# All four batches' projections by Strassen's product, one batch behind the attention; the cluster mask of the first six pairs as a one-hot product on TensorE

## The chip, the cores and the metric

The kernel runs on one core of a Trainium2 chip, in one launch. The metric is the device time of an execution in microseconds (us), lower is better. TensorE, VectorE, ScalarE, GpSimd and SyncE appear in the profile as PE (its weight loads as PEld), DVE, ACT, POOL and SP; a q behind a name (SPq, POOLq) is the engine's DMA queue.

## The reference, cut to what matters

```python
# q, k, v: (4, 8, 768, 64) float32; centroids: (8, 16, 64) float32
q_n = q / (norm(q) + 1e-6); k_n = ...; c_n = ...          # unit vectors
q_assign = argmax(einsum('bhsd,hcd->bhsc', q_n, c_n)); k_assign = ...
mask   = q_assign[:, :, :, None] == k_assign[:, :, None, :]
scores = where(mask, (q @ k.T) / sqrt(64), -1e9)
attn   = softmax(scores)                                   # row by row
x = (attn @ v), heads side by side                         # (3072, 512)
h = x @ w_in                                               # w_in  (512, 2048) float64
g = h - tanh(h)
out = g @ w_out                                            # w_out (2048, 512) float64
```

A query attends only to the keys of its own cluster. The weights arrive as 64-bit floats, two 32-bit words each, and the kernel makes float32 of them itself.

## The kernel before, in words

**Attention.** Two heads make a pair, one on partitions 0 to 63 and one on 64 to 127; four batches of four pairs make 16 pairs. Of a pair, the 768 queries are taken in two halves of 384, and the 768 keys in six blocks of 128. Two key blocks are one *step*, so there are 3 steps in a half, 6 in a pair, 24 in a batch and 96 in all. A step's work: eight score matmuls (`score`, L327; a float32 matmul has two records in the trace), an exponential of both blocks on ACT in place in PSUM (L332), the cluster mask on DVE (`select`, L341: exponential times "query's code equals key's code", from PSUM into the SBUF tile `e`), sums of `e` over the keys on Pool (L350 for the first two blocks, L354 twice in each later step), and the product with the values on PE (`value`, L363). There are two PSUM buffers for scores and two for `e`.

**Ends of a half.** `take` copies the result from PSUM (L386), `total` multiplies Pool's sums by ones on PE (L396), ACT adds an epsilon (L400), Pool adds to a check tile (L401, `wholes`), `divide` takes the reciprocal in three parts on DVE (L407), multiplies (L410), and Pool adds to another check tile (L411, `inverses`). In the first half of batch 0 (`early`) Pool sums nothing: PE multiplies `e` by ones in every step (L372).

**Stages of the next pair.** q and k are loaded, transposed on PE (L248) and copied on ACT (L255); similarities to the centroids (L267, L272), transposes (L280), four DVE operations that give each row a cluster code (L286 to L293), a transpose and a cast of the queries' codes (L302, L306), a DMA that writes them to DRAM (L308), and one for each half that spreads them over all partitions (L315, tile `row`).

**Projections.** One batch's attention runs while the projections of the batch before run between its instructions. For batch 0 they are plain products: `plain_items(0)` and `plain_items(1)` for the two halves of the queries, up (L424), tanh (L429), difference (L431), down (L439). To begin early, batch 0 takes all first halves (steps 0 to 11) and then all second halves (12 to 23); half 0 is projected in steps 12 to 23 and half 1 in steps 24 to 47. Batches 1 to 3 use Strassen's product with seven multiplications for eight: `up_pair` (L599, then DVE additions L585, tanh L589, Pool L590, L623, L624) and `down_product` (L641, DVE L652, Pool L648, L661). Batch 1 is projected in steps 48 to 71, batch 2 in 72 to 95, and batch 3 after the last step (the tail).

**Weights.** `weights_on` turns 32 pieces of 512 KB into float32 during the first 24 steps: a DMA on Pool's queue (L164), ACT (L120), and three DVE operations (`assemble`: L121, L125, L128). They stay in SBUF until batch 0 is projected. From step 24 on, `up_maker` and `down_maker` form the sums of Strassen's factors on DVE (L516) and write all factors to DRAM; they are streamed back for each batch (L538). From step 48 on, the weights are read again for a range check (L732, L742).

The order is written out by hand: `steps` lists the steps, `fills` which projection runs beside them, `ready` the stages of later pairs, `makers` the factor work, and `todo` holds a step's small work, dealt out between the items of the projection by `between`. In one turn of the loop PE gets the next step's scores first, then this step's values:

```python
            if following:
                begin(following)
            value(n, half, s)
```

Of the kernel before, what the change touches and what calls it, by code (L numbers as in the profile page):

```python
# [30 lines left out]
F32 = mybir.dt.float32  # L31
# [20 lines left out]

@with_exitstack
def kernel(
# [42 lines left out]
    smallest = const.tile([P, 2 * len_pieces], F32, name="smallest")  # L97
    flag = const.tile([1, 1], I32, name="flag")
# [13 lines left out]

    def assemble(dst, raw, rest):
# [5 lines left out]
        lo, hi = pair[:, :, 0], pair[:, :, 1]  # L119
        nc.scalar.activation(out=rest, in_=lo, func=ACT.Copy, scale=2.0**-29)  # L120
# [9 lines left out]
    def fast():  # L130
# [4 lines left out]
        codep = cx.enter_context(tc.tile_pool(name="codep", bufs=6))  # L135
        qbp = cx.enter_context(tc.tile_pool(name="qbp", bufs=3))
# [8 lines left out]
        first = ExitStack()  # L145
        vp0 = first.enter_context(tc.tile_pool(name="vp0", bufs=2))
        turnp0 = first.enter_context(tc.tile_pool(name="turnp0", bufs=2))
        wp = first.enter_context(tc.tile_pool(name="wp", bufs=1))
        gp = first.enter_context(tc.tile_pool(name="gp", bufs=CF // 2))
        thp = first.enter_context(tc.tile_pool(name="thp", bufs=2))  # L150
        outp = first.enter_context(tc.tile_pool(name="outp", bufs=2))
        rawp = first.enter_context(tc.tile_pool(name="rawp", bufs=3))
        w_in = [wp.tile([P, CD, FQ * P], F32, name=f"w_in{i}") for i in range(NQ4)]
        w_out = [wp.tile([P, FQ, DM], F32, name=f"w_out{i}") for i in range(NQ4)]
        PIECES = pieces(w_in, w_out)
        raws = {}

        def fetch_weights(n: int):
            dst, src = PIECES[n]
            if words == 1:  # L160
                nc.gpsimd.dma_start(dst, src)
                return
            raws[n] = rawp.tile([P, 2 * FQ * P], U32, name="raw")
            nc.gpsimd.dma_start(raws[n], src)  # L164

        def round_weights(n: int):
            if words == 1:
                return
            rest = outp.tile([P, FQ * P], U32, name="rest", tag="osb")
            assemble(PIECES[n][0], raws.pop(n), rest)  # L170

        def constants():
            make_identity(nc, ident)
            nc.vector.memset(ones, 1.0)
            nc.vector.memset(inverses, 0.0)
            nc.vector.memset(wholes, 0.0)
            for c in range(C):
                nc.vector.memset(down[:, c : c + 1], float(C - c))

        cen = const.tile([P, D], F32, name="cen")  # L180
# [4 lines left out]
        def centroid_norms():  # L185
# [7 lines left out]
            nc.scalar.sqrt(nrm, ss)  # L193

# [25 lines left out]


# [3 lines left out]
        def load(n: int, what=(0, 1)):  # L225
# [3 lines left out]
            for i in what:  # L229
                if i < 2 and b == 0:  # L230
                    t = raw_qk[n, i] = gp.tile([P, NCH, 2, D], F32, name=f"x{i}", tag="g")
                elif i < 2:
                    t = raw_qk[n, i] = loads.tile([P, NCH, 2, D], F32, name=f"x{i}")
                else:
                    pool = vp0 if n in (2, 3) else vp
                    t = vals[n] = pool.tile([P, 2, NCH, D], F32, name="vals")
# [6 lines left out]
        def turn(n: int, i: int, engine):  # L243
# [8 lines left out]
            pool = turnp0 if n in (2, 3) else turnp  # L252
            t = turned[n, i] = pool.tile([P, 2, TB], F32, name=f"t{i}")
# [43 lines left out]

        def publish(n: int):

            G = HCH * 4  # L300
            ps = ps_f.tile([G, P], F32, name="pq", tag="f")
            nc.tensor.transpose(  # L302
                out=ps, in_=codes[n][:, 0].rearrange("p a h j -> p (a h j)"), identity=ident
# [75 lines left out]
        def early(n: int, half: int):  # L379

            return n < HP and half == 0
# [684 lines left out]
```

## Time and profile before

| what | value |
|---|---|
| median of 3 runs (lowest, highest) | 1077.87 us (1077.58, 1079.89) |
| the profiled execution, its own time | 1080.79 us |
| its span in the profile, instructions | 1078.9 us, 11996 |
| PE, DVE, ACT, POOL busy | 1007.2, 622.4, 300.7, 551.6 us |
| granted TensorE clock, mean | 0.982 |
| moved by DMA | 124.68 MB |

The profile shows one execution. Busy times are unions of an engine's instructions; the idle time of an engine that doesn't set the pace costs nothing. Matmuls overlap each other, so the mean duration of one is longer than the time that it adds.

### The profile page before, as it was taken

Reading aid. Unit: us, or ns where it says so; the run is one execution under the profiler, and the core shown is the slowest. Engines: PE = TensorE matmul, PEld = TensorE weight load, DVE = VectorE, ACT = ScalarE, POOL = GpSimd, SP = SyncE. Lnnn points to the kernel's source line nnn. Section 1 sums busy time; section 2 is a strip of 40 time slices with the busy share of each in tenths; the row PEclk is TensorE's granted clock in tenths of the full one; section 3 lists DMA queues with packets and bytes.
Section 4 is the critical chain, followed back from the end, with each engine's and each line's share of the span. In section 5 each row is a group of like instructions: output and inputs, shape, how many; then the busy total and the mean of one; then the engine's idle time right before and its main releaser. Section 6 shows DMA issues by size and latency. Waiting matters only on the chain.

```text
span 1078.9 us, 11996 instructions
## 1 busy us (share of the span) xinstructions
PE 1007.2 (93%) x4258; PEld 557.9 (52%) x4258; DVE 622.4 (58%) x1100; ACT 300.7 (28%) x458; POOL 551.6 (51%) x398
## 2 busy tenths in 40 slices
PE   4787998999999999999999999999999999799996
PEld 2332444444444444444456666544456666456885
DVE  5688999335776757656655546655754435544011
ACT  3443433223343323333232221333242211122000
POOL 1012454344655555576678435576778535446701
PEclk9899999999999999999999999999999999899999
DMA  9342343104253352543453454534221222223320
GB/s 261 106 115 84 115 139 93 47 18 124 81 162 108 117 178 89 185 136 112 135 170 131 146 164 141 164 115 144 101 101 49 98 88 74 92 74 112 127 93 32
DMA packets 101603, 124.68 MB, mean 116 GB/s; under 512 B 55328, under 2 KB 80928, under 8 KB 98848
## 3 DMA queue, kind: packets, MB, share of 16 engines
q1 hardware_dynamic: 94576, 100.73, 30.3%
q0 software_dynamic: 6816, 23.07, 6.5%
q8 instruction: 36, 0.59, 0.2%
q14 instruction: 31, 0.25, 0.1%
q10 hardware_dynamic: 144, 0.03, 0.0%
HBM read 102.79 MB, written 21.02 MB: 115 GB/s over the span
## 4 chain that ended last, share of the span: by engine, by line
PE 75%; DVE 10%; issue 7%; POOL 3%; SPq 2%; ACT 2%; DMA 1%; POOLq 0%; DVEq 0%; ACTq 0%
PE pu L599 19%; PE pd L641 14%; PE sc L327 12%; PE av L363 11%; PE o L439 8%; PE h L424 6%; DVE e L341 3%; SPq L238 2%; PE den L396 2%; PE pt L248 2%; PE sim L267 1%; DVE den L407 1%; DVE w_out L125 1%; PE den L372 1%; POOL G L661 1%
## 5 line engine op out<-in xcount | busy, mean ns | idle before, releaser
L341 DVE SCALAR_TENSOR_TENSOR e<-row,code,sc 128x384 f32<-128x384 bf16 x384 | 211.6, 608 | 124.4 <-ACT sc L332 105.2
L354 POOL TENSOR_TENSOR sum<-sum,e 128x768 f32<-128x768 f32 x112 | 207.9, 1856 | 94.4 <-DVE e L341 90.1
L332 ACT ACTIVATE sc<-sc 128x768 f32<-128x768 f32 x192 | 145.1, 790 | 202.1 <-PE sc L327 201.2
L641 PE MATMUL pd<-stream,G 128*128 128x256 f32 x864 | 193.9, 382 | 1.4 <-POOL G L590 1.4
L641 PEld LDWEIGHTS pd<-stream,G 128*128 128x128 f32 x864 | 162.0, 190 | 36.1 <-issue 12.0
L327 PE MATMUL sc<-t,t 64*128 64x384 f32 x768 | 156.6, 519 | 25.1 <-DVE e L341 22.7
L363 PE MATMUL av<-e,vals 128*64 128x384 f32 x768 | 149.5, 512 | 0.0
L599 PE MATMUL pu<-xT,stream 128*128 128x384 f32 x384 | 138.9, 498 | 0.0
L590 POOL TENSOR_TENSOR G<-G,th 128x768 f32<-128x768 f32 x48 | 86.5, 1822 | 89.5 <-ACT th L589 85.1
L327 PEld LDWEIGHTS sc<-t,t 64*128 64x128 f32 x768 | 66.4, 187 | 100.2 <-issue 63.9
L599 PEld LDWEIGHTS pu<-xT,stream 128*128 128x128 f32 x384 | 71.7, 192 | 59.3 <-issue 11.2
L599 PE MATMUL pu<-diff,stream 128*128 128x384 f32 x288 | 101.0, 486 | 0.3 <-DVE diff L565 0.3
L350 POOL TENSOR_TENSOR sum<-e 128x768 f32<-128x768 f32 x28 | 53.6, 1916 | 80.1 <-DVE e L341 80.1
L363 PEld LDWEIGHTS av<-e,vals 128*64 128x64 f32 x768 | 47.7, 139 | 90.0 <-issue 88.2
L424 PE MATMUL h<-xT,w_in 128*128 128x384 f32 x256 | 89.8, 502 | 3.2 <-DVE g L431 3.2
L407 DVE RECIPROCAL den<-den 128x128 f32<-128x128 f32 x96 | 83.1, 915 | 8.2 <-POOL wholes L401 8.2
L439 PE MATMUL o<-w_out,g 128*128 128x512 f32 x192 | 87.6, 602 | 0.0
L589 ACT ACTIVATE th<-G 128x768 f32<-128x768 f32 x48 | 39.8, 843 | 149.2 <-DVE G L585 140.6
L599 PEld LDWEIGHTS pu<-diff,stream 128*128 128x128 f32 x288 | 54.2, 190 | 38.2 <-DVE diff L565 1.0
L424 PEld LDWEIGHTS h<-xT,w_in 128*128 128x128 f32 x256 | 47.6, 192 | 45.1 <-issue 8.7
L657 POOL DMA_DIRECT2D out_dram<-c x36 | 19.9, 554 | 83.9 <-DVE c L652 83.6
L411 POOL TENSOR_TENSOR inverses<-inverses,den 128x384 f32<-128x384 f32 x32 | 41.5, 1297 | 37.6 <-DVE den L407 36.7
(100 smaller groups left out, 867.0 us busy)
## 6 DMA issues: line engine op xcount, KB each, us to landing
stream<-up_factors SPq DMA_DIRECT2D x24, 896.0 KB
stream<-down_factors SPq DMA_DIRECT2D x21, 1024.0 KB
raw<-in_moe_w_in_dram POOLq DMA_DIRECT2D x16, 512.0 KB, 4.5
raw<-in_moe_w_out_dram POOLq DMA_DIRECT2D x16, 512.0 KB, 4.3
again<-in_moe_w_in_dram SPq DMA_DIRECT2D x32, 256.0 KB
again<-in_moe_w_out_dram SPq DMA_DIRECT2D x32, 256.0 KB
x<-in_q_dram SPq DMA_DIRECT2D x32, 192.0 KB
x<-in_k_dram SPq DMA_DIRECT2D x32, 192.0 KB
```

The source lines that it names most:

```text
L327: nc.tensor.matmul(sc[:, h, 0:TB], lhsT=turned[n, 1][r].rearrange("p a n -> p (a n)")[:, j * P : (j + 1) * P], rhs=turned[n, 0][r, half], ...
L332: nc.scalar.activation(out=sc[:, :, 0:TB], in_=sc[:, :, 0:TB], func=ACT.Exp, scale=SCALE)
L341: nc.vector.scalar_tensor_tensor(out=e[:, h], in0=rows[n, half][:, h], scalar=codes[n][:, 1, j // HCH, h, j % HCH : j % HCH + 1], in1=sc[: ...
L350: nc.gpsimd.tensor_tensor(out=s, in0=pair[:, 0], in1=pair[:, 1], op=ALU.add)
L354: nc.gpsimd.tensor_tensor(out=s, in0=s, in1=pair[:, i], op=ALU.add)
L363: nc.tensor.matmul(avs[n, half][h * D : h * D + D], lhsT=vals[n][:, h, j], rhs=e[:, i, h], start=(j == 0), stop=(j == NCH - 1),)
L407: nc.vector.reciprocal(out=t[:, c], in_=t[:, c])
L424: nc.tensor.matmul(h, lhsT=w_in[i][:, c, o * P : (o + 1) * P], rhs=xT[c][:, half], start=(c == 0), stop=(c == CD - 1),)
L439: nc.tensor.matmul(acc[sub], lhsT=gs[f % HF][:, f // HF, sub * P : (sub + 1) * P], rhs=w_out[f // FQ][:, f % FQ], start=(f == sequence[0]) ...
L590: nc.gpsimd.tensor_tensor(out=g[:, f].rearrange("p a n -> p (a n)"), in0=g[:, f].rearrange("p a n -> p (a n)"), in1=th.rearrange("p a n -> ...
L599: nc.tensor.matmul(ps, lhsT=streams[base + i][:, k_, c], rhs=right[which][c], start=(c == 0), stop=(c == CH - 1),)
L641: nc.tensor.matmul(ps, lhsT=left[:, i], rhs=t[:, i], start=(i == 0), stop=(i == HF - 1))
```

## The change

- Batch 0 also goes through Strassen's product. `plain_items`, `early` and the half-by-half order of batch 0 go. Batch b is projected in the 24 steps of batch b + 1 for b = 0, 1, 2, batch 3 in the tail. Steps 0 to 23 have no projection beside them. `fetch_factors` streams factors for all four batches.
- The 32 pieces are rounded and summed as eight units, during the two calls before the loop and steps 0 to 26 (`MADE`): `round_piece` (two raw buffers in place of three), `sum_of`, and one `keep` for each unit, which stores seven factors in one DMA in a new layout.
- For the first six pairs (`masked`) the select on DVE goes. The codes of queries and keys are both spread over the partitions; `one_hot` makes 1 where a query's code is the partition's, and -2^100 where a key's code is not; a bf16 product of the two is added to the scores in PSUM, and the exponential writes straight to `e`.
- Pool sums `e` in all halves, batch 0's first ones too. The rows of a pair are spread once, not once for each half.
- G, the left factors and the late pools are split in two halves that are opened at different times; two Pool subtractions in the down products become two each.
- At the start `keep_warm` runs matmuls of zeros, and the weights' first DMAs wait (`gate`) for pair 0's k. In the tail two more up products come before the transpose of the check's result. The check also reads q and k of the first six pairs again (`largest`).

The diff, cut to its core:

```diff
+MASKED = 6
+FAR = 2.0**100
...
+        def keep_warm(times: int):
+            ps = ps_f.tile([P, 2 * P], F32, name="warm", tag="f")
+            for _ in range(times):
+                nc.tensor.matmul(
+                    ps, lhsT=inverses[:, 0:P], rhs=inverses[:, 0 : 2 * P], start=True, stop=True
+                )
...
+        def one_hot(n: int):
+            t = rows[n]
+            nc.vector.tensor_scalar(
+                out=t[:, 1], in0=t[:, 1], scalar1=mine_code, scalar2=-FAR,
+                op0=ALU.not_equal, op1=ALU.mult,
             )
+            nc.vector.tensor_scalar(
+                out=t[:, 0], in0=t[:, 0], scalar1=mine_code, scalar2=None, op0=ALU.is_equal
+            )
...
+        def begin(step):
...
+                if masked(n):
+                    for h in range(2):
+                        r = slice(h * D, h * D + D)
+                        nc.tensor.matmul(
+                            sc[i][:, h, 0:TB],
+                            lhsT=rows[n][r, 1].rearrange("p a n -> p (a n)")[:, j * P : (j + 1) * P],
+                            rhs=rows[n][r, 0, half], start=False, stop=True,
+                        )
+                    if i == 0:
+                        weights[n, half, s] = ep.tile([P, 2, 2, TB], F32, name="e")
+                    out = weights[n, half, s][:, i]
+                else:
+                    scores[n, half, j] = sc[i]
+                nc.scalar.activation(out=out, in_=sc[i][:, :, 0:TB], func=ACT.Exp, scale=SCALE)
...
-            if j % 2 == 1 and not early(n, half):
+            if j % 2 == 1:
                 pair = weights[n, half, j // 2]
...
+        def round_piece(at: int):
+            if words == 2:
+                rest = restp.tile([P, FQ * P], U32, name="rest")
+                assemble(queue[at][0], raws.pop(at), rest)
+            fetch(at + 2)
...
+        def keep(m: int):
+            t, q_, r = units.pop(m), m % 4 // 2, m % 2
+            if m < HF // 2:
                 nc.sync.dma_start(
+                    up_factors[q_ * FQ : (q_ + 1) * FQ, :, r].rearrange("i p k f -> p i (k f)"),
+                    t[:, :, 0:7].rearrange("p i k f -> p i (k f)"),
+                )
...
+        makers = []
+        for m in range(8):
+            makers += [lambda at=4 * m + i: round_piece(at) for i in range(4)]
+            makers += [lambda m=m, k_=k_: sum_of(m, k_) for k_ in range(4)]
+            makers += [lambda m=m: keep(m)]
...
-        steps = [(p, half, s) for half in range(2) for p in range(HP) for s in range(NS)] + [
-            (n, half, s) for n in range(HP, len(pairs)) for half in range(2) for s in range(NS)
-        ]
+        steps = [(n, half, s) for n in range(len(pairs)) for half in range(2) for s in range(NS)]
...
+        PLACES = (0, 1, 1, 2, 3, 4)
...
-        fills = {HALF: (lambda: plain_items(0), HALF), 2 * HALF: (lambda: plain_items(1), 2 * HALF)}
-        for b in range(1, B - 1):
-            fills[2 * (b + 1) * HALF] = (lambda b=b: strassen_items(b), 2 * HALF)
+        fills = {2 * (b + 1) * HALF: b for b in range(B - 1)}
+        MADE = 2 * HALF + NS
...
             if makers:
-                share = -(-len(makers) // max(4 * HALF - 2 - at, 1))
+                share = -(-len(makers) // max(MADE - at, 1))
                 todo += makers[:share]
...
         fine = const.tile([P, 1], F32, name="fine")
         nc.vector.tensor_reduce(out=fine, in_=wholes, axis=AX.X, op=ALU.min)
+        for it in tail[2:4]:
+            it[2](lambda: None)
```

## The prediction, made before the changed kernel ran

> **What bounds the kernel now.** I read the page first, then the windows view cut at the steps of the loop, then the groups by form, and last the timeline of one stretch. The cuts are the starts of the first exponential (L332) of steps 0, 12, 24, 48 and 72 and of the last step. The columns are each engine's busy time, the granted TensorE clock, the DMA share and GB/s.
>
> ```profile
> 0.00:27.60 27.60, 11.05 (x56) 5.73 (x56) 14.44 (x55) 9.00 (x13) 4.02 (x12) 1.00 1.05 264
> 27.60:108.60 81.00, 62.02 (x317) 25.59 (x317) 62.86 (x107) 32.25 (x49) 12.92 (x17) 0.89 0.33 101
> 108.60:237.70 129.10, 123.00 (x446) 56.49 (x448) 90.05 (x139) 42.35 (x71) 56.41 (x45) 0.99 0.28 84
> 237.70:419.40 181.70, 180.76 (x746) 80.46 (x744) 120.18 (x180) 61.32 (x96) 98.53 (x59) 1.00 0.40 118
> 419.40:662.70 243.30, 236.92 (x1050) 136.73 (x1048) 146.22 (x275) 69.97 (x105) 153.62 (x104) 0.99 0.47 148
> 662.70:895.70 233.00, 227.57 (x1002) 132.60 (x1000) 131.86 (x241) 65.76 (x98) 151.17 (x103) 0.99 0.32 105
> 895.70:1078.90 183.20, 165.93 (x649) 120.27 (x645) 56.81 (x107) 20.10 (x31) 74.97 (x60) 0.97 0.25 88
> ```
>
> From step 12 on PE (first busy column) is busy 95 to 99% until the tail: a step that has a projection beside it lasts as long as its matmuls. Steps 0 to 11, which have none, take 6.75 us each with PE at 77% and DVE at 78%; no engine is full, they hand work to each other. So the change must be priced by two rules: PE time where a projection runs, and the other engines where none does.
>
> The groups that the sums use (busy, then mean ns of one):
>
> ```profile
> L341 DVE SCALAR_TENSOR_TENSOR e<-row,code,sc 128x384 f32<-128x384 bf16 x384 | 211.6, 608 | 124.4 <-ACT sc L332 105.2 <-issue 8.8 <-POOL G L590 5.1
> L354 POOL TENSOR_TENSOR sum<-sum,e 128x768 f32<-128x768 f32 x112 | 207.9, 1856 | 94.4 <-DVE e L341 90.1
> L424 PE MATMUL h<-xT,w_in 128*128 128x384 f32 x256 | 89.8, 502 | 3.2 <-DVE g L431 3.2
> L439 PE MATMUL o<-w_out,g 128*128 128x512 f32 x192 | 87.6, 602 | 0.0
> L372 PE MATMUL den<-e,ones 128*64 128x384 f32 x96 | 17.7, 489 | 0.0
> ```
>
> And five rows of the timeline, in which the same two DVE operations of `assemble` run once with Pool quiet and once with Pool adding:
>
> ```profile
> 128.62 0.42 DVE L121 TENSOR_SCALAR w_out<-raw 128x512 uint32<-128x512 uint32 x1
> 129.08 0.69 DVE L125 SCALAR_TENSOR_TENSOR w_out<-raw,w_out 128x512 uint32<-128x512 uint32 x1
> ...
> 132.26 3.78 POOL L354 TENSOR_TENSOR sum<-sum,e 128x768 f32<-128x768 f32 x2 [1.42 <-DVE e L341]
> ...
> 133.55 0.82 DVE L121 TENSOR_SCALAR w_out<-raw 128x512 uint32<-128x512 uint32 x1
> ...
> 134.40 2.19 DVE L125 SCALAR_TENSOR_TENSOR w_out<-raw,w_out 128x512 uint32<-128x512 uint32 x1
> ```
>
> L125 takes 0.69 us alone and 2.19 us here: Pool's second addition ends at 132.26 + 3.78 = 136.04, L125 at 136.59, 0.55 us later. L125 waited for Pool's whole addition. L341, which reads `sc` from PSUM, takes 608 ns either way. So DVE work between SBUF tiles and Pool's additions take turns. That decides this change: it takes L341, which shares nothing, out of the first 24 steps, and puts Pool's additions beside all of `assemble` and the factor sums.
>
> **PE time, all stages.** Out: the plain products, 89.8 + 87.6 = 177.4 us, and L372, 17.7. In: Strassen's products of one batch. In the page's groups up is 138.9 + 101.0 for three batches, 80.0 for one; down is 193.9 for the records with G and, at the same price, a sixth of that for those with S: 226.2, 75.4 for one. Together 155.4: 22.0 less. L396 for four more halves adds 4 x 0.86 = 3.4. The mask products have no row. Eight score records, which are four float32 products of the same shape, take 1.56 us in a step. If a bf16 product is one such record it is half of that, 0.78; if that record is also half as long, 0.39, my lower end; the upper one is 1.56. I take 0.5, near the lower end, as an estimate: 36 steps x 0.5 = 18. Net on PE: -177.4 - 17.7 + 155.4 + 3.4 + 18 = -18.3 us. If every microsecond were PE's, that would be the gain. It isn't, since batch 0's attention loses its cover.
>
> The Trainium skill (TensorE: Matmul & The Clock Gate, "Measured speedup vs the span model" and "Back-to-back issue gap") has products on different rows of the array run together, for the time of one and some 4 ns, and a warm bf16 gap of 162 ns for 384 columns. By an estimate from that page a step's masks would be 0.33 us and the 18 would be 12.
>
> **Start (27.6 before).** The first exponential now waits for the mask, so for the chain codes, DRAM, row: in the timeline the cast at 23.4 leads to the write's DMA at 25.39, the read's at 29.88 and the row at 32.8, 9.4 us. Before it, the centroid chain is moved ahead of the transposes and the weights' DMAs wait, so the cast comes some 7 us earlier (q landed at 6.8, and PE then waited until 13.9 for the centroids). 16.4 + 9.4 = 25.8: **26**, from 24 to 30.
>
> **Steps 0 to 23 alone.** The end of this stretch is the exponential of step 24, which needs `one_hot(4)` of step 22 on DVE and Pool's sum of step 22. What must be done by then, from the rows in their quiet durations:
> - Pool: a half is 5 additions of 1.80, `wholes` 0.99, `inverses` 1.00: 11.0; eight halves less the last step 84. Its DMA issues (0.55 each) need no turn.
> - DVE between SBUF tiles: `makers` gives three items in each of steps 0 to 15 and then two, so some 27 pieces x (0.42 + 0.69 + 0.69) = 48.6, 28 factor sums of half of L516's 1.21 = 17.0, L410 7 x 0.56 = 3.9, L291 4 x 0.56 = 2.2, eight `one_hot` operations. For these no row has bf16 in and out: L121 (0.42 for 512 numbers) is nearest; for 768 of half the size I take its 0.42, from 0.2 to 0.85: 3.4. Sum 75.
> - DVE that shares nothing: reciprocals 7 x 2.74 = 19.2, codes and casts 4 x 1.94 = 7.8. These 27 hide under Pool.
>
> In turn that is 84 + 75 = 159. As an L125 ends 0.55 and not 0.69 after Pool, each of the 128 DVE operations hides 0.14 of itself, 18 in all: 141. Neither is reached: Pool's queue also holds the DMA of each new piece, which waits until DVE is done with an old one, and then its sums stand behind it; and ACT's L120 waits for a raw buffer with the next exponential behind it. I take **153**, between them and nearer the upper end. PE needs less: 24 x (1.56 + 1.51 + 0.5) + 8 x 0.86 + 4 x 3.7 (L248, L267, L280, L302) = 107, or 120 at the 0.89 clock of the second window; ACT some 73. The spread of pair n is three steps ahead of its use, so the 9.4 us chain is covered at 6.4 us a step, as SP's queue holds one `keep` in nine items before it.
>
> A rule of the Trainium skill speaks against this stretch from another side. The second window keeps a granted clock of 0.89 with PE 77% busy. The same page ("What's actually happening") has only full and half rate, half after an idle window of some 3.4 us. PE at half rate throughout would be 214 by that, and set the pace.
>
> **Steps 24 to 47.** As steps 48 to 71 today, 243.3, plus 12 masked steps x 0.5 = 6 on PE. L341's 12 x 2.43 = 29 on DVE goes, worth nothing, as DVE is 60% busy there. Added in front: today plain products (L439) run until 425.6 while the last division and the differences (L565) are made; now PE has only scores and values to do, and DVE two pieces in between: 4 us of waiting, from 0 to 10, the SP queue with the first factors behind a `keep` included. **253.** Steps 48 to 71 and 72 to 95 keep **243.3** and **233.0**: the single spread, the split subtractions and 24 more reads and reductions (0.41 each) lie beside full PE.
>
> **Tail (183.2).** PE's 6.66 us wait for `fine` (L879) and the slow clock behind it (eight matmuls in 4.54 in place of 2.74) are filled by two up products. DVE's 6 us chain stays, and three PSUM buffers cover four products of it, 5.5 us. **177**, from 175 to 181.
>
> Sum: 26 + 153 + 253 + 243.3 + 233.0 + 177 = 1085.3, 6.4 over the span of 1078.9. The profiled execution took 1080.79, 1.9 over its span and 2.9 over the median; I carry the 6.4 to the median: **1084.3**. All turns on steps 0 to 23: 146.6 is the point of no change.
>
> **Rivals.**
> - *Pool and DVE fit together* (faster). Pool's additions fall into DVE's 27 us of reciprocals and codes and into its waits, or the pieces are done quicker: the stretch is between PE's 120 and the 141, at 134 say, and the time 1065; at 120 it is 1051. For it: DVE loses its 58 us of L341 there. Against it: this needs a port never empty.
> - *Lockstep* (much slower). Pool, DVE and the raw DMA (4.4 us to landing, two buffers) run in series. Three steps are then DVE 15 (four pieces, four sums, a division, half a route) + Pool 11 less 3.5 hidden, 22.5, or 7.5 a step: 180 and 1111. It decides once a piece waits for its DMA. The 6.75 of today's uncovered steps is the nearest row, and gives 162 and 1093.
> - *The mask is dear.* At 1.56 a step the 12 masked steps beside the projection cost 13 us more: 1097.
>
> **How the numbers follow.** Forecast 0.45 (1078 to 1097), fit 0.35 (1050 to 1077), lockstep 0.14 (1095 to 1115), dear mask 0.06. The range 1054 to 1106 leaves out the quickest fit and the slowest lockstep. Within 0.2%, which is what a measurement here can tell from nothing, lie 2.2 us on either side, at the seam of forecast and fit: 0.06; faster 0.36, slower 0.58.
>
> **What would show it.** In the windows by step: 0 to 23 near 153 with PE near 70%, L125 and L128 well above 0.69, and Pool's L164 waiting for DVE; 24 to 47 near 253; the tail without the 6.66. I am wrong if the first stretch is under 146, or if its idle time is charged to DMA.

## The result, and the profile after

| | before | changed |
|---|---|---|
| median of 4 runs (lowest, highest) | 1078.88 us (1077.58, 1084.0) | 1110.37 us (1109.56, 1112.56) |
| profiled execution: time, span | 1080.79, 1078.9 us | 1109.68, 1107.9 us |

The ratio is 1.0286 (95% interval 1.0248 to 1.0324). The forecast was 1084.3 with a range of 1054 to 1106: the sign was right, the size was not. The rival "lockstep" named 1111. Two executions stand far off and enter no ratio below: one of e13 with 3508.75 us and one of e14 with 2545.59.

The windows view of the changed kernel, cut at the first exponential (now L390) of steps 0, 24, 48, 72 and of the last step; the columns are those of the view of before:

```profile
0.00:31.60 31.60, 17.20 (x71) 11.78 (x71) 13.61 (x57) 5.61 (x9) 3.09 (x11) 0.86 0.82 205
31.60:203.30 171.70, 118.83 (x598) 48.34 (x596) 146.23 (x162) 66.24 (x101) 105.22 (x79) 0.81 0.54 175
203.30:453.70 250.40, 237.29 (x1084) 138.41 (x1084) 139.21 (x231) 70.86 (x106) 159.55 (x113) 0.98 0.44 143
453.70:698.20 244.50, 239.79 (x1074) 141.40 (x1072) 149.23 (x281) 69.28 (x103) 157.21 (x113) 0.99 0.44 141
698.20:928.40 230.20, 225.73 (x1002) 132.05 (x1000) 128.98 (x230) 65.76 (x98) 151.88 (x108) 1.00 0.28 92
928.40:1107.90 179.50, 165.92 (x649) 120.13 (x645) 57.50 (x109) 20.03 (x31) 76.65 (x66) 0.97 0.26 90
```

| stretch | forecast | measured | miss |
|---|---|---|---|
| start | 26 | 31.6 | +5.6 |
| steps 0 to 23 | 153 | 171.7 | +18.7 |
| steps 24 to 47 | 253 | 250.4 | -2.6 |
| steps 48 to 71 | 243.3 | 244.5 | +1.2 |
| steps 72 to 95 | 233.0 | 230.2 | -2.8 |
| tail | 177 | 179.5 | +2.5 |

Two rows carry the miss. In steps 0 to 23 no engine but DVE is near full: DVE 146 of 171.7 us (85%), PE 119 (69%), Pool 105. The groups of this stretch alone, by form:

```profile
L413 POOL TENSOR_TENSOR sum<-sum,e 128x768 f32<-128x768 f32 x31 | 59.9, 1933 | 11.1 <-ACT e L390 9.8
L533 DVE TENSOR_TENSOR unit<-unit 128x512 f32<-128x512 f32 x28 | 40.1, 1460 | 0.4
L141 DVE SCALAR_TENSOR_TENSOR unit<-raw,unit 128x512 uint32<-128x512 uint32 x26 | 23.4, 899 | 0.9
L452 DVE TENSOR_TENSOR xT<-xT,den 128x384 f32<-128x384 f32 x7 | 11.2, 1604 | 0.2
L350 DVE TENSOR_SCALAR row<-row,mine_code 128x768 bf16<-128x768 bf16 x4 | 7.6, 1905 | 0.1
```

L533 are the factor sums, L452 is the multiplication of `divide`, L350 one of the two operations of `one_hot`. Their means are 2.0, 2.9 and 4.6 times what they take with Pool's additions gone (0.72, 0.56 and 0.42 us in the first experiment). They don't wait at a semaphore, so the time counts as busy. One place in the timeline shows what happens, and whom it makes late:

```profile
112.58 2.60 DVE L533 TENSOR_TENSOR unit<-unit 128x512 f32<-128x512 f32 x1
112.81 4.03 POOL L413 TENSOR_TENSOR sum<-sum,e 128x768 f32<-128x768 f32 x2
115.10 1.95 DVE L350 TENSOR_SCALAR row<-row,mine_code 128x768 bf16<-128x768 bf16 x1
116.98 0.41 DVE L354 TENSOR_SCALAR row<-row,mine_code 128x768 bf16<-128x768 bf16 x1
...
117.44 0.82 PE L380 MATMUL sc<-row 64*128 64x384 bf16 x4 [7.20 <-DVE row L354]
```

Pool adds from 112.81 to 116.84. L533 waits for the first addition, L350 behind it for the second, and only when Pool is done does L354 run at its own 0.41 us. PE has stood for 7.2 us by then. The Trainium skill (SBUF — State Buffer, "SBUF: two separate sides") gives the rule: a DVE operation that has two inputs in SBUF, or that runs in a mode with two ports, and a Pool operation that reads SBUF, as these additions do, share a pair of ports, which goes to whichever starts first, for its whole instruction; the other waits. The rows agree that it is a wait and not a shared rate: the four L350 of this stretch take 1.95, 1.95, 1.95 and 1.77 us, and each ends 0.21 to 0.23 us after the Pool addition beside it, the last one shorter because it began later in that addition. Which of the two started first can't be read off the records, though: L533's record here begins 0.23 us before Pool's, and yet L533 is the one that waits; at 43.26 and 89.40 an L533 with the same lead takes 0.69 us.

The same stretch in the view of waits (us in total, times, longest):

```profile
PE sc L380 <- DVE row L354: 20.9, 3, 7.2
PE pq L320 <- DVE code L306: 17.9, 4, 6.6
...
ACT rest L136 <- DMA raw<-in_moe_w_out_dram: 13.9, 5, 4.7
...
DVE unit L144 <- ACT rest L136: 11.0, 3, 8.4
...
DVE den L449 <- POOL wholes L444: 4.3, 1, 4.3
...
DVE unit L137 <- DMA raw<-in_moe_w_out_dram: 4.1, 3, 2.0
```

The last three rows are most of the 25.5 us in which DVE has nothing to do (171.7 less 146.2). No row has ACT waiting for Pool to be done with a tile `e`, so the trace gives no sign that the additions cost time in that way; PE waits 4.5 us for the sums themselves.

### The profile page after: what moved, and what is told of

Its sections match the earlier page's. It is cut to its first block, busy times and chain, and to the rows that moved or that the text cites. A ratio compares the mean times of both kernels' runs of the same rounds, so it can differ in the third digit from the quotient of the medians.

```text
span 1107.9 us, 12424 instructions
## 1 busy us (share of the span) xinstructions
PE 1004.8 (91%) x4468; PEld 592.1 (53%) x4468; DVE 634.8 (57%) x1067; ACT 297.8 (27%) x447; POOL 653.6 (59%) x487
## 4 chain that ended last, share of the span: by engine, by line
PE 65%; DVE 15%; issue 8%; DMA 4%; POOL 3%; SPq 2%; ACT 2%; POOLq 0%; DVEq 0%; ACTq 0%
PE pu L640 23%; PE pd L686 20%; PE av L422 9%; PE sc L369 9%; DVE unit L533 2%; DMA raw<-in_moe_w_out_dram 2%; PE den L439 2%; DVE den L449 2%; SPq L252 2%; DVE unit L144 1%; PE pt L262 1%; DVE unit L141 1%; DVE unit L137 1%; DVE e L400 1%; DVE G L626 1%
## 5 line engine op out<-in xcount | busy, mean ns | idle before, releaser
L413 POOL TENSOR_TENSOR sum<-sum,e 128x768 f32<-128x768 f32 x128 | 238.8, 1865 | 51.4 <-DVE e L400 33.6
L686 PE MATMUL pd<-stream,G 128*128 128x256 f32 x1152 | 259.4, 382 | 1.4 <-POOL G L631 1.4
L686 PEld LDWEIGHTS pd<-stream,G 128*128 128x128 f32 x1152 | 215.5, 190 | 47.6 <-issue 16.1
L640 PE MATMUL pu<-xT,stream 128*128 128x384 f32 x512 | 185.8, 498 | 1.9 <-DMA stream<-up_factors 1.9
L400 DVE SCALAR_TENSOR_TENSOR e<-row,code,sc 128x384 f32<-128x384 bf16 x240 | 133.3, 608 | 74.3 <-ACT sc L390 69.6
L640 PE MATMUL pu<-diff,stream 128*128 128x384 f32 x384 | 138.0, 495 | 8.8 <-DVE diff L604 6.7
L390 ACT ACTIVATE sc<-sc 128x768 f32<-128x768 f32 x120 | 90.5, 789 | 179.3 <-PE sc L369 171.8
L390 ACT ACTIVATE e<-sc 128x768 f32<-128x768 f32 x72 | 54.3, 806 | 91.3 <-PE sc L380 90.9
L626 DVE TENSOR_TENSOR G<-pu,u 128x384 f32<-128x384 f32 x96 | 52.6, 550 | 23.5 <-PE pu L640 23.5
L626 DVE TENSOR_TENSOR u<-pu,u 128x384 f32<-128x384 f32 x64 | 35.2, 550 | 45.6 <-PE pu L640 45.4
```

The lines of the kernel that those rows point to most:

```text
L390: nc.scalar.activation(out=out, in_=sc[i][:, :, 0:TB], func=ACT.Exp, scale=SCALE)
L400: nc.vector.scalar_tensor_tensor(out=e[:, h], in0=rows[n][:, half, h], scalar=codes[n][:, 1, j // HCH, h, j % HCH : j % HCH + 1], in1=sc[: ...
L413: nc.gpsimd.tensor_tensor(out=s, in0=s, in1=pair[:, i], op=ALU.add)
L626: nc.vector.tensor_tensor(out=out, in0=x, in1=y, op=ALU.add)
L640: nc.tensor.matmul(ps, lhsT=streams[base + i][:, c, k_], rhs=right[which][c], start=(c == 0), stop=(c == CH - 1),)
L686: nc.tensor.matmul(ps, lhsT=of(i), rhs=t[:, i], start=(i == 0), stop=(i == HF - 1))
```

## The experiments

Three theories at first. **Turns**: Pool's additions and DVE's operations take the port in turn, and this alone makes steps 0 to 23 long. **Raw DMA** (the lockstep rival): the pieces wait for their DMA, in series with both. **No cover**: one batch of attention by itself can't go quicker than 7.15 us a step. Later the question was what remains when Pool is quiet. The kernels of before in the same jobs had medians of 1079.7 to 1081.0 us. "Stretch" is steps 0 to 23 of one profiled execution. That matters where a kernel's executions differ: those of e1 lie between 1074.65 and 1082.61 us (profiled: 1075.38), of e2 between 1076.18 and 1086.31 (profiled: 1086.31, the longest), of e7 between 1064.54 and 1079.36 (profiled: 1069.27), of e18 between 1074.48 and 1089.34 (profiled: 1080.33). Differences of a few us between their stretches show nothing.

| run | what differs | median us | ratio to before (interval) | stretch |
|---|---|---|---|---|
| e1_sums_pe | batch 0's sums of e on PE | 1079.43 | 0.9995 (0.9976 to 1.0014) | 143.7 |
| e2_sums_out | 32 of Pool's 40 additions left out | 1080.15 | 0.9996 (0.9978 to 1.0015) | 149.0 |
| e3_raw3 | third raw buffer | 1108.71 | 1.0277 (1.0253 to 1.03) | 172.1 |
| e4_late | 27 items after step 23 | 1107.88 | 1.0258 (1.0237 to 1.028) | 146.7 |
| e5_codes | pair 0's codes asked first | 1103.12 | 1.0221 (1.0196 to 1.0245) | 171.9 |
| e7_joined | e1, e3 and e5 | 1070.29 | 0.9909 (0.9883 to 0.9935) | 143.2 |
| e8_mask4 | e7, four masked pairs | 1063.80 | 0.9851 (0.9831 to 0.9871) | 136.6 |
| e9_nomask2 | mask on DVE again | 1122.58 | 1.0393 (1.0373 to 1.0413) | 202.1 |
| e10_idle | e1's products, Pool's sums stay | 1119.43 | 1.036 (1.0344 to 1.0377) | 181.9 |
| e11_mix | e8, Pool sums second halves | 1080.11 | 1.0001 (0.9987 to 1.0016) | 150.4 |
| e12_acts | e1, ACT copies for DVE's sums | 1095.68 | 1.0128 (1.0089 to 1.0167) | 159.9 |
| e13_lesspe | e1, a third of PE's sums | 1078.01 | 0.9972 (0.9953 to 0.999) | 142.6 |
| e14_order | codes ahead of the pieces | 1114.03 | 1.0293 (1.0244 to 1.0343) | 179.2 |
| e15_best | e8 with e14's order | 1066.42 | 0.9865 (0.9829 to 0.99) | 143.1 |
| e16_noload | two pieces loaded, 30 not | 1099.83 | 1.0172 (1.015 to 1.0194) | 169.9 |
| e17_noload_pe | e1 with e16's edit | 1066.61 | 0.9872 (0.9852 to 0.9893) | 138.6 |
| e18_norest | e1, ACT's low words left out | 1082.86 | 1.0018 (0.9991 to 1.0044) | 143.4 |

**e1_sums_pe.** PE multiplies `e` by ones in batch 0, as the kernel before did for its first halves; Pool adds nothing there.

```diff
-            if j % 2 == 1:
+            if j % 2 == 1 and not early(n):
...
+            if early(n):
...
+                for i in range(2):
+                    for h in range(2):
+                        nc.tensor.matmul(
+                            sums[n, half][h * D : h * D + D], lhsT=ones, rhs=e[:, i, h],
+                            start=(s + i == 0), stop=(2 * s + i == NCH - 1),
+                        )
+
+        def early(n: int):
+
+            return n < HP
```

These are four products a step; the trace has two records for each, and the "eight" of the texts on record, here and for the scores, counts records.

> Batch 0's sums of e go from Pool to PE in both halves (eight matmuls with ones in each of steps 0 to 23, 1.46 us a step by L372 of the kernel before); everything else is as in the changed kernel. Steps 0 to 23 took 171.7 us there, the execution 1110.4. Theory 'turns' (Pool's additions and DVE's operations between SBUF tiles exclude each other, DVE falls behind, the codes and the one-hot come late and PE waits for them): the 40.1 us of factor sums (L533, 1460 ns each) fall to some 17 (600 ns), DVE's 146 busy us in the stretch to some 107, the stretch to 135 to 150 although PE gets 28 us more, the time to some 1080. Rival 'raw DMA' (pieces wait for their 512 KB, 20 us of the chain): those waits stay or grow, the stretch is at least 165, the time at least 1100. Rival 'no cover' (one batch of attention by itself hands work round PE, ACT and PE and can't go quicker than 7.15 us a step): PE's extra work lengthens it, time 1125 to 1140.

The window of its stretch, then its groups of factor sums and of `one_hot`:

```profile
29.50:173.20 143.70, 127.73 (x754) 55.00 (x752) 106.91 (x164) 66.36 (x101) 30.64 (x41) 0.96 0.66 216
```

```profile
L548 DVE TENSOR_TENSOR unit<-unit 128x512 f32<-128x512 f32 x28 | 19.2, 717 | 0.4
L350 DVE TENSOR_SCALAR row<-row,mine_code 128x768 bf16<-128x768 bf16 x4 | 1.7, 416 | 1.1 <-DMA row<-q_codes 1.1
```

DVE falls from 146.2 to 106.9 with the same operations: 39 us of its busy time had been Pool's. The stretch falls by 28.0, the time by 31: the whole loss against before hangs on these 40 additions. At 5.99 us a step 'no cover' falls too.

**e2_sums_out.** The second to sixth key blocks' additions (32 of 40) are left out in batch 0, nothing put in their place.

```diff
-                else:
+                elif n >= HP:
                     s = sums[n, half]
```

> Left out of the computation: four of the five additions of e on Pool in each half of batch 0 (L413; L409 stays), so nothing takes their place on PE. Theory 'turns': factor sums at 600 to 800 ns, the stretch of steps 0 to 23 at 120 to 140 in place of 171.7, the time 1060 to 1080. Rival 'raw DMA': 155 or more and 1095 or more. Rival 'no cover': no change, 1110.

```profile
32.70:181.70 149.00, 111.33 (x600) 46.43 (x600) 113.14 (x164) 66.40 (x102) 46.68 (x49) 0.86 0.63 204
```

149.0, more than expected, with PE at 111 us. It is more than e1's 143.7 too, but that is not shown to be a difference: this was the longest of eight executions, and the medians, 1080.15 and 1079.43, are level. So the additions are the loss (22.7 us for 32), but something else keeps the stretch far above what PE and DVE need.

**e3_raw3.** Three raw tiles, each fetched three ahead; the late pool `s` gets one buffer for two to make room.

```diff
-        rawp = making.enter_context(tc.tile_pool(name="rawp", bufs=2, side="right"))
+        rawp = making.enter_context(tc.tile_pool(name="rawp", bufs=3, side="right"))
...
-            fetch(at + 2)
+            fetch(at + 3)
...
```

> Three raw buffers and pieces fetched three ahead in place of two (one of the two late buffers of s pays for the space; each up product writes s once and has read it long before the next). Theory 'turns': the waits for raw data go (22 us of ACT's, 15 of DVE's idle time in front of L144), but part of that time is then spent waiting for Pool: the stretch 160 to 168, the time 1099 to 1106. Rival 'raw DMA': the stretch 145 to 152, the time 1084 to 1091. Rival 'no cover': 1110.

172.1: nothing, although ACT's wait for raw pieces fell from 22.0 to 14.6 us. Against raw DMA, and the 160 to 168 of turns was missed as well.

**e4_late.** 45 items before step 24, the other 27 in steps 24 to 29.

```diff
-                share = -(-len(makers) // max(MADE - at, 1))
+                if at < 2 * HALF:
+                    share = -(-max(len(makers) - 27, 0) // (2 * HALF - at))
+                else:
+                    share = -(-len(makers) // max(2 * HALF + 6 - at, 1))
```

> Of the 72 items that make the factors 45 are done up to step 23 and 27 in steps 24 to 29, beside the first projections, in place of 60 and 12; nothing is left out. DVE has some 18 items less in steps 0 to 23, about 8 pieces and 8 sums, by the changed kernel's rows 8 x 2.30 + 8 x 1.46 = 30 us. Theory 'turns' (DVE sets the stretch): 138 to 148 for steps 0 to 23, 250 to 260 for 24 to 47, the time 1080 to 1092. Rival 'raw DMA': a quarter of the waits go, 5 to 8 us, 1102 to 1106. Rival 'no cover': 1110.

The stretch shrank by 25 as turns has it, and the window behind it took it all back (277.2 where it was 250.4):

```profile
180.60:457.80 277.20, 246.43 (x1084) 141.73 (x1084) 168.38 (x264) 76.26 (x116) 164.73 (x120) 0.94 0.50 161
```

There too Pool adds, and DVE is busy for 168.4 us where it was 139.2. Up to 260 us of the trace ACT waits 19.5 us for the `G` that DVE makes for the projection, 7.5 in the changed kernel, and PE waits 6.4 for the first factors, where it was 1.9. Moving the work moved the loss; the 250 to 260 us and the 1080 to 1092 that turns forecast for this were missed.

**e5_codes.** In the start, the loads of pairs 2 and 3 and the values of pair 1 are asked after pair 0's codes and rows.

```diff
-        load(2)
-        load(1, (2,))
-        load(3)
...
         spread(0)
+        load(2)
+        load(1, (2,))
+        load(3)
```

> The changed kernel with the loads of pairs 2 and 3 and pair 1's values asked for after pair 0's codes and rows, not before, on SP's queue. In the changed kernel the codes were ready at 15.3 us and their DMA was issued at 21.4, behind those loads, and the first exponential began at 31.6. Theory 'queue' (SP's queue held the codes): the DMA at 15.5 to 16.5, the first exponential at 25 to 27, everything behind it unchanged, the time 1104 to 1106. Rival: the loads that are now later, or the transfers that still run, hold the rows as long, the exponential at 30 to 32 and the time 1110.

The start of the changed kernel, then of this one (timeline, single rows):

```profile
15.01 0.28 DVE L324 CAST qc<-pq 24x128 bf16<-24x128 f32 x1 [0.45 <-PE pq L320]
...
17.45 3.85 SPq L252 DMA_DIRECT2D x<-in_k_dram  x2
21.42 0.70 SPq L326 DMA_DIRECT2D q_codes<-qc  x1
```

```profile
15.15 0.39 SPq L326 DMA_DIRECT2D q_codes<-qc  x1
```

The codes were cast at 15.3 and lay until 21.4 behind loads on SP's queue. Without these the start is 24.7 in place of 31.6.

**e6_nomask** was to undo the mask, but left `one_hot(0)` in the start, so pair 0 selected on spoiled codes and the launch went on to the general path: 4976 us. Its steps 0 to 23 took 204.1 us in the trace (the next expectation says 196.5).

> The mask part of the change undone by itself: no pair is masked on TensorE, all selects are on DVE, the rest as in the changed kernel (the check on q and k is left out with it). Theory 'turns' with DVE setting the pace of steps 0 to 23: DVE gets 24 x 2.43 = 58 us and loses some 10 of one-hots and waits, the stretch goes from 171.7 to 205 to 220, steps 24 to 47 lose 6 us of mask products at most, the time 1138 to 1155. Rival 'dear mask' (the one-hot product and its wait cost as much as they save): 1105 to 1115.

**e9_nomask2** undoes the mask properly: the select on DVE for all pairs.

```diff
-MASKED = 6
+MASKED = 0
...
-        one_hot(0)
+        if masked(0):
+            one_hot(0)
```

> The mask part undone by itself, now with pair 0's rows left as they are too (before, its rows still went through the one-hot, the sums came out as nothing and the launch went on to the general path; its first part had taken 196.5 us for steps 0 to 23). Theory 'turns' with DVE setting the pace: the stretch at 190 to 205, steps 24 to 47 and the rest as with four masked pairs (246, 243, 230, 179), the time 1118 to 1130. Rival 'dear mask': 1110 or less.

As expected: the mask costs 12.1 us in the start (19.5 without it) and saves 30.4 in the stretch, where DVE would be at 186 us. The mask is not dear.

**e7_joined** is e1, e3 and e5 together.

> Three edits together, nothing left out: batch 0's sums on PE (this alone: stretch 143.7, time 1079.4), three raw buffers (alone: nothing), and the codes ahead of the later loads. Theory: with Pool's additions gone the waits for raw data (23 us of ACT's idle time in the stretch with the sums on PE) are no longer hidden behind waits for Pool, so the third buffer now pays: stretch 130 to 138, start 26 to 28 in place of 29.5, the time 1064 to 1072. If the raw data was never what held the pieces: stretch 143, only the start gains, 1075 to 1077.

1070.29, faster than before by 0.9%. The start is 24.3; the stretch, 143.2, is e1's again: the third raw buffer gives nothing in it even with Pool quiet, and the 130 to 138 of the theory was missed. The time came 5 to 7 us under the 1075 to 1077 of the rival, which had the stretch right.

**e8_mask4** masks by product in pairs 0 to 3 only; pairs 4 and 5 lie beside the projection and take DVE's select.

```diff
-MASKED = 6
+MASKED = 4
```

> As the joined kernel, with the mask product for the first four pairs and not six. Theory: beside a projection PE sets the pace, so the 12 steps of pairs 4 and 5 lose 12 x 0.5 = 6 us of PE while their selects (29 us) fall on DVE's free time there: steps 24 to 47 go from 247.7 to some 242, the time 4 to 6 under the joined kernel. Rival (DVE is late in steps 24 to 30, as in the kernel that moved 27 items there): no gain or a loss of up to 10.

1063.80, the fastest of all, 1.5% below before. The median is 6.5 us under e7's, 4 to 6 were expected, but the place was not: steps 24 to 47 gave 1.1 us, steps 0 to 23 gave 6.6. Why there, no run settles, and e7's own executions differ by more than that (its shortest is 4.7 us under the profiled one). PE is now busy for 124.3 of the 136.6 us.

**e10_idle** asks whether e1 was faster because a busier PE keeps its clock. e1's products run, their result is not read, and Pool's sums stay.

```diff
+            if n < HP:
+                idle = ps_f.tile([P, TB], F32, name="idle", tag="f")
+                for i in range(2):
+                    for h in range(2):
+                        nc.tensor.matmul(
+                            idle[h * D : h * D + D], lhsT=ones, rhs=e[:, i, h], start=(i == 0), stop=(i == 1),
+                        )
```

> The changed kernel, Pool's sums left where they are, plus the same eight matmuls with ones in each of steps 0 to 23 that moved the sums to PE, with a result that nothing reads. It has the PE work and the busy clock of the kernel with the sums on PE, and Pool's additions. In that kernel the stretch took 143.7 us at a granted clock of 0.96, in the changed one 171.7 at 0.81. Theory 'turns': Pool's additions were what cost; the clock rises here too, to 0.9 or more, but the stretch stays at 165 to 175 and the time at 1103 to 1113. Rival 'clock' (PE was slow because it was too idle, and its own load cured that): the stretch falls to 145 to 152, the time to 1083 to 1090.

```profile
33.10:215.00 181.90, 144.06 (x782) 60.55 (x780) 149.83 (x164) 66.31 (x101) 107.24 (x80) 0.88 0.53 170
```

The clock rose from 0.81 to 0.88 and the stretch too, by 10 us, above both theories. Against e1, with the same PE work, it is 38.2 us longer: that difference is Pool's additions. A higher clock did not shorten the stretch; what the slow spells of the clock by themselves cost is not shown.

**e11_mix** is e8 with Pool summing the second halves of batch 0: 20 additions.

```diff
+        def early(n: int, half: int):
+
+            return n < HP and half == 0
```

> As the joined kernel with four masked pairs (1063.8 us, stretch 136.6 with PE busy 124.3), but only the first halves' sums of batch 0 on PE; Pool sums the second halves. Theory 'turns' with PE as the pace-maker of that kernel's stretch: PE loses 17.5 and gains 3.4, 14 us; DVE waits for 20 additions of 1.8 us, at the changed kernel's rate (146 - 107 = 39 us of waits for 40 additions) 20 us more on 107, still under PE; the stretch 125 to 140, the time 1052 to 1067. Rival 'clock': PE less busy runs slower, the stretch 140 to 150, the time 1067 to 1077.

150.4, slower by 13.8 in the stretch, though PE has 7 us less to do. So PE was not the pace-maker there, and the 125 to 140 was missed. The clock rival's 140 to 150 is near, but 20 additions at the 0.70 us that e1 gave for one are 14 us without it.

**e12_acts, e13_lesspe**, both on e1, take work from one engine: in e12 ACT copies where DVE added factors; in e13 PE sums in the last step of a half only.

```diff
-            nc.vector.tensor_tensor(out=part(SLOT[which]), in0=part(x), in1=part(y), op=op)
+            nc.scalar.copy(out=part(SLOT[which]), in_=part(x))
```

```diff
-            if early(n):
+            if early(n) and s == NS - 1:
...
```

> Built on the kernel with batch 0's sums of e on PE (its steps 0 to 23 took 143.7 us, PE 127.7, DVE 106.9, ACT 66.4 busy). One edit more: where DVE made a sum of two factors (28 of them in the stretch, 19.2 us), ACT copies one of the two; the factors are therefore not Strassen's, only the time is meant. If DVE's queue sets the rest of the stretch, it falls by most of the 19: 126 to 132. If PE and the hand-over of scores do, it stays at 141 to 146, and if ACT's queue does, whose exponentials then stand behind the copies, it rises above 147.

> Built on the kernel with batch 0's sums of e on PE (steps 0 to 23: 143.7 us, PE 127.7). One edit more: PE sums only the last two key blocks of each half in batch 0, so 64 of the 96 sum products go and the divisors hold a third of the keys. If PE's work sets the rest of the stretch, it falls by what those products took, 64 at about 0.17 us of PE time: to 132 to 135. If DVE or the hand-over does, it stays at 141 to 146; if a busier PE had only kept its clock up, it rises to about 149, as in the kernel without Pool's additions.

With 20 us less on DVE and 15 more on ACT the stretch grew by 16; with 14 us less on PE it stayed:

```profile
33.40:176.00 142.60, 113.27 (x626) 47.66 (x624) 106.17 (x164) 66.27 (x101) 30.32 (x41) 0.89 0.66 211
```

So PE's amount of work does not set what is left. e12 does not acquit DVE, since the copies stand in front of exponentials on ACT.

**e14_order, e15_best** put the next pair's codes and their spread ahead of the step's pieces and sums, on the changed kernel and on e8.

```diff
+            todo += [stages[i] for i in (2, 3) if i in stages]
             if makers:
...
-            todo += [stages[i] for i in (2, 3) if i in stages]
```

> The changed kernel, with the cluster codes of the next pair and their spread put ahead of the step's pieces and factor sums in the list of small work, nothing else. DVE takes its work in order, and in the changed kernel PE waited 18 us for the codes and 31 us for the one-hots. If it is this order that lengthens the stretch beyond the 153 of the forecast, steps 0 to 23 fall from 171.7 to 155 to 162 and the time to about 1097. If DVE is simply late by the whole of its held-up work, the order only moves the wait to the next scores: 168 to 172, and the time stays at 1107 to 1111.

> The fastest version so far (sums of batch 0 on PE, three raw buffers, pair 0's codes asked first, four masked pairs: 1063.8 us, steps 0 to 23 in 136.6) with the codes put ahead of the step's pieces and sums as well. PE is 91% busy in that stretch, so little is left: 133 to 137, and 1060 to 1064, if the order costs anything; the same 136 to 137 if PE itself is the limit now.

Both grew, by 7.5 and 6.5, which neither branch of either expectation had. (The 31 us of waiting for one-hots that e14's expectation names include 10.3 before step 0; in the stretch it is 20.9.) In e14 PE's wait for codes no longer stands among the large ones, but ACT's wait for raw pieces went from 22 to 53 us with the next exponential behind it: being early with one thing in an in-order queue makes another late.

**e16_noload, e17_noload_pe** fetch the first two of the 32 pieces only and make all others from them, on the changed kernel and on e1.

```diff
+            if at >= 2:
+                raws[at] = held[at % 2]
+                return
...
```

> The changed kernel, but only the first two of the 32 weight pieces are fetched; all others are made from these two tiles, so the factors are wrong numbers, and only the time is meant. In the changed kernel ACT waited 22 us and DVE 4 us for raw pieces, with exponentials behind ACT's wait. The lockstep rival (raw DMA in series with Pool and DVE): steps 0 to 23 fall from 171.7 to 145 to 152. Pool's additions alone make the stretch long: it stays at 165 to 172.

> The same on the kernel with batch 0's sums on PE (steps 0 to 23: 143.7), where ACT waited 23 us for raw pieces. If the raw pieces set the rest that Pool's additions leave, the stretch falls to 122 to 130; if it is the hand-over of scores between the engines' queues, it stays at 138 to 144.

```profile
29.00:198.90 169.90, 116.51 (x600) 47.73 (x598) 148.09 (x162) 65.77 (x102) 94.19 (x53) 0.81 0.30 98
```

```profile
28.30:166.90 138.60, 128.35 (x757) 55.58 (x754) 106.56 (x164) 66.25 (x102) 16.20 (x14) 0.95 0.36 120
```

With no piece to wait for, the stretch keeps 169.9 of 171.7 (first row). Raw DMA falls. With Pool quiet (second row) it gives 5.1. The loads cost elsewhere too: e16's time is 10.5 us under the changed kernel's, 2.6 of it in the start, 2.2 in steps 24 to 47 and 2.8 in the tail, and e17's is 12.8 under e1's, with its four executions within 1.3 us.

**e18_norest**, on e1: ACT makes the low words of the first two pieces only.

```diff
+        if low:
             nc.scalar.activation(out=rest, in_=lo, func=ACT.Copy, scale=2.0**-29)
```

> The kernel with batch 0's sums on PE (steps 0 to 23: 143.7), with all loads, but ACT makes the low words of the first two pieces only and the others take these, so ACT's queue holds exponentials without anything in between that waits for a DMA; the factors are wrong in their low bits, only the time is meant. DVE waited 19 us for ACT's low words there, and ACT 23 us for raw pieces. If this exchange between ACT's and DVE's queues is what holds the stretch above the 107 to 120 of the forecast's terms, it falls to 122 to 132; if not, it stays at 140 to 144.

143.4: no change, in one trace of a kernel whose executions differ by 15 us. The wait of DVE for ACT (18.8 us) is gone, and DVE waits 16 us for the spread codes and 10 for PE's transposes in its place.

## Why the prediction was right or wrong

**Right: what decides, and which way.** The forecast said that Pool's additions and DVE's SBUF work take turns, that this decides steps 0 to 23, and that the point of no change is 146.6. e1 takes the additions away: 143.7 and a time level with before. Four pairs of kernels give a price for one addition: 22.7 / 32 = 0.71 (e2), 28.0 / 40 = 0.70 (e1), 13.8 / 20 = 0.69 (e11 against e8), 31.3 / 40 = 0.78 (e16 against e17). With PE's work held equal (e10 against e1) it is 38.2 / 40 = 0.96. The medians of the times, which don't hang on one execution, give 0.94, 0.77, 0.82, 0.83 and 1.00. An addition of 1.93 us costs 0.7 to 1.0 us.

**Wrong: "I take 153" for steps 0 to 23.** The step took 159 (Pool's 84 and DVE's 75 in turn) and 141 (18 of it hidden) for its two ends. Seen from DVE, the 141 is 102 of its own work, 75 and 27, and 39 in which it is held: Pool's 84 less the 27 that lie under it less the 18. So 153 leaves at most 12 us for the waits that the step names, Pool's queue and ACT's wait for a raw buffer. Measured, with e1's DVE time for its own work: 106.9 own, 39.3 held and 25.5 idle, together 171.7. Own work and turns were priced about right. The term that was mis-sized is DVE's idle time: 25.5 us where at most 12 were left for it, so at least 13.5 of the 18.7 that the stretch missed by. The turns fell on other operations than forecast: 21 of the 39 us on the factor sums, while L144, the L128 of before, kept 0.72 us, though it was to rise well above 0.69.

Said from the other side: without any addition the forecast's own terms make the stretch 107 to 120 (PE) or 102 (DVE). It is 149.0 in e2 and 142.6 in e13, whose PE has little or nothing more to do (111 and 113 us); in e1, e7, e8, e17 and e18 PE makes the sums as well, and it is 136.6 to 143.7. The forecast had the sign for it in view, 6.75 us a step with PE 77% and DVE 78% busy, and named 162 from that row, but only under a rival. A stretch in which engines hand work to each other was priced as if one of them were nearly full.

Why DVE is idle for so long is not settled. Each of these, taken out on e1, left the stretch within 5.1 us: 14 us of PE's work, 30 of the 32 raw loads, the low words that ACT makes for 30 pieces. As one wait went, DVE's next instruction waited for something else. DVE's amount of work was not tested by itself.

**Lockstep's number, not its trigger.** 1111 was its price and 1110.4 came. Its trigger, a piece that waits for its DMA, is refuted by e16; its 22.5 us for three steps would have made 180, and 171.7 was measured. The misses in the other stretches made up the difference: that the number met is luck.

**Start, 26.** The cast came earlier than forecast (15.0 for 16.4), but the 9.4 us chain was taken from a place where SP's queue was ahead of it. Here loads held the write's DMA until 21.4, 6.1 us after the cast (in the kernel before it left at 25.39, 1.7 us after), and the chain took 15.2 us, from 15.0 to the first `one_hot` at 30.25. With the loads behind it (e5) it took 8.7. The 1.4 us from there to the exponential had no term in the sum. e5 gives 6.9 us back.

**The codes in the loop** were said to be covered at 6.4 us a step. They weren't: PE waited 17.9 us for the codes and 20.9 for `one_hot` in the stretch. It was DVE's queue, not SP's, that was late: its idle time before L350 in the stretch is 0.1 us in all.

**Right in size:** `one_hot`, 0.42 us quiet (0.42 taken from L121), and up to 1.95 beside Pool. The mask products, four of them 0.49 us from the first one's start to the last one's end (0.5 taken), 0.82 where PE had just waited; the dear mask falls. What they add is less: the records of the two on different rows start 7 ns apart and those of the next two 0.16 us later (at 208.7 us in the trace), and with them gone from 12 steps (e8 against e7) PE's busy time in steps 24 to 47 fell by 1.95 us, not by 6. Steps 24 to 47: 6.4 us of PE waiting for the differences and 1.9 for the first factors, where 4 in all were taken; the total still came 2.6 lower. Tail: the wait of 6.7 us for `fine` is gone; 2.1 for a `G` came in.

**The clock.** The stretch ran at a granted 0.81, where the forecast bounded half rate throughout at 214. In the view of windows the clock is 1.00 from 57.0 to 66.8 us and 0.50 from 67.0 to 77.0, and in the timeline the eight score records of a step take 1.56 us in some steps and 2.93 in others, full and about half rate. The Trainium skill (TensorE: Matmul & The Clock Gate, "What's actually happening") has only these two in that section; a mean of 0.81 would then be some 38% of the time at half rate, an estimate from that page. e10 and e13 speak against the clock as what sets the length of the stretch: in e10 it is higher and the stretch longer, in e13 lower (0.89 against e1's 0.96) and the stretch the same.

## What to carry to other kernels

Count Pool's additions and those DVE operations that they hold as one resource, and expect the delay to show as longer DVE instructions, not as waits. Here that was the additions and products of two SBUF tiles, the operations of `assemble` and `one_hot`; reciprocals (0.88 to 0.95 us) and reductions (0.54 to 0.56 us) took the same beside Pool's additions and without them. Where no engine is full, do not add up busy times and call the sum an upper end: take the time of a step from the nearest uncovered stretch (6.75 us, 162 for 24 steps, was nearer here than 153), and ask of each in-order queue what stands behind its next wait. Before work is moved into a stretch, see what covered it where it was: here a product on PE, which had room, was the better place for the sums (1063.8 us with it).

## What was not expected of the hardware

- Without Pool's additions the times of one kernel can lie further apart (e1 1074.65 to 1082.61, e2 1076.18 to 1086.31, e7 1064.54 to 1079.36) than those of the changed kernel (1109.56 to 1112.56), but not in all such kernels (e8 1062.45 to 1064.70, e17 1066.52 to 1067.76). No run shows why.
- Four more products a step (e10: PE busy for 144.1 us, from 118.8) raised the granted clock from 0.81 to 0.88.
- Two thirds of the sum products less (e13) took 14 us from PE's busy time and the clock from 0.96 to 0.89; the stretch did not notice.
